# A linear-attention and MLP block on one core: tile 3 turned through memory, three tiles normalised on ScalarE, and the first tiles' small work put in other places

## The chip, the cores and the metric

The kernel runs on one core of one Trainium2 chip. The metric is the device time of one execution in microseconds (us), the median of several runs. A profile of one execution stands beside it; its times are those of the span from the first to the last instruction.

## The reference, cut to what matters

`x` has 2048 rows (tokens) of 512 floats. The rows are normalised, and two branches that both read the normalised rows are added to `x`:

```python
xn = layernorm(x)                                  # per row: (x - mean) / sqrt(var + 1e-5)
q, k, v = split(xn @ wqkv)                         # 32 heads of 16
phi = lambda t: where(t > 0, t + 1, exp(t)) + 1e-6
kv, z = phi(k)^T v, sum(phi(k))                    # per head, over all tokens
a = (phi(q) kv / (phi(q) z + 1e-6)) @ wo
b = relu(xn @ w1 + b1) ** 2 @ w2 + b2              # 512 -> 1376 -> 512
out = x + a + b
```

## The kernel before

**Tiles and stages.** The 2048 tokens are 16 tiles of 128 (`NT`), four to a block (`TB`). The change lies in the first stage, which goes over the tiles once. For each tile i this stage normalises the rows (`xp[i]`), turns them so that the features lie on the partitions, splits the turned tile into a rounded high part and a remainder (`xs..h`, `xs..l`), multiplies by the k weights (`project`, 12 matmuls of 128x512, line 368), applies phi (`phi_k`, lines 359 to 363), splits phi(k) the same way (`parts`, lines 375 and 376), splits the normalised rows themselves (`tokens`, `tok`, lines 111 and 119), and adds the product of tokens and phi(k) to four sums (`kx`, 12 matmuls, line 388). Splitting always means: ScalarE copies the high part, then VectorE (in `tokens` mostly GpSimd) subtracts it from the source. The later stages (from about 94 us on) make the MLP and the attention out of these results.

**Two ways to turn a tile.** Tiles below `NDVE` (0 to 3 before) are turned by four TensorE transposes against an identity (`turned_pe`, line 307), from PSUM. From `NDVE` on a tile is turned "by moves": `normalise` writes `xp[i]` in groups of 32 columns, `regroup` (line 280) stores it into a DRAM buffer `via`, `move` (line 288) loads it back in four pieces into `xg`, and `turn` (line 292) transposes 32x32 blocks on VectorE. Tiles 4 and 5 make the trip singly (`xg4s`, two places), tiles 6 and 7, 8 and 9 and so on in pairs. `transposed(i)` does either and gives back three pieces of work: `high` (line 323, ScalarE), `low` (line 326, VectorE) and `keep_t`, which stores the turned tile to DRAM as `xTd` for a later stage (line 335), for tiles below `NDVE` after a ScalarE copy out of PSUM.

**Statistics and normalising.** `measure` (lines 233 and 234, VectorE) gives mean and variance, `roots` (lines 244 and 245, GpSimd, the addition for tiles 0, 1 and 6 on VectorE) gives the inverse deviation. `normalise` works on VectorE for tiles below `NPE` = 8 (line 267); from 8 on it first makes `u = -mean * r` (line 253, VectorE) and gives back ScalarE work (`last`, line 257).

**Order.** There is no scheduler: the order of the calls is the order on each engine, and an engine works its queue strictly in order. All loads, stores and moves of this stage go through one queue, that of SP, also in order; an SP instruction that waits holds up all later ones. The lines 576 to 661 spell out tiles 0 to 3. The loop over i from 2 (line 806) then issues, per turn: `move()`, `project(i)`, for i < `NDVE` the turning of tile i + 1, `phi_k(i)` with `mid` (after its first ScalarE instruction) and `late` (after its second) as places for `high` and `low`, `parts(i)`, `tokens(i + 1)`, the put-off normalising `later`, the turning of tile i + 2, the statistics, and `kx(i - 1)`. `ones(i)` (line 345, GpSimd) sets the last feature column of a tile to 1 once nobody needs its value. `load_x` (line 158) loads raw rows: tiles 4 to 7 in one load, 8 to 15 in four loads of 512 KB.

TensorE's order between 16 and 40 us is thus: kx(0), the transposes of tile 3, kx(1), project(3), kx(2), project(4), kx(3), project(5), kx(4), project(6).

Of the kernel before, what the change touches and what calls it, by code (L numbers as in the profile page):

```python
# [7 lines left out]
F32 = mybir.dt.float32  # L8
F32R = mybir.dt.float32r
AF = mybir.ActivationFunctionType  # L10
OP = mybir.AluOpType
# [7 lines left out]
def kernel(  # L19
# [39 lines left out]
    BT = TB * P  # L59
    NF = -(-F // P)  # L60
    NPE = 2 * TB
    NDVE = NPE - 4
    WARM = 11
    NP = NF // 2
    FP = NF * P
# [25 lines left out]
    def two(name):  # L91
        return keep.tile([P, 2, 512], F32, name=name, tag=next_tag("x"))
# [7 lines left out]
    def f32(ap):  # L100
        return ap.bitcast(F32)
# [7 lines left out]
    def copy(eng, o, i, bias=0.0):  # L109
        if eng == "act":  # L110
            nc.scalar.activation(o, i, AF.Copy, bias=bias)  # L111
        elif bias:
            ENG[eng].tensor_scalar(o, i, bias, None, op0=OP.add)
        else:
            ENG[eng].tensor_copy(o, i)

    def split(h, l, src, eh, el):
        copy(eh, h, src)
        ENG[el].tensor_tensor(out=l, in0=src, in1=f32(h), op=OP.subtract)  # L119
# [36 lines left out]
    def load_x(i, t):  # L156
        n = t.shape[1]
        nc.sync.dma_start(t, xf[i * P:(i + n) * P, :].rearrange("(i p) d -> p i d", i=n))
        for k in range(n):
            xr[i + k] = t[:, k]  # L160
# [68 lines left out]
    def measure(g, *ks):  # L229

        tiles, st, mv, _ = g
        for k in ks or range(len(tiles)):
            nc.vector.bn_stats(st[:, k, :], xr[tiles[k]])  # L233
            nc.vector.bn_aggr(mv[:, k, :], st[:, k, :])

    def statistics(*tiles):
        g = group(*tiles)
        measure(g)
        return g

    def roots(tiles, st, mv, y):

        n = len(tiles)
        (nc.vector if tiles[0] in (0, 1, 6) else nc.gpsimd).tensor_scalar(y[:, 1, :n], mv[:, :n, 1], 1e-5, None, op0=OP.add)
        nc.gpsimd.tensor_tensor(out=y[:, 0, :n], in0=y[:, 1, :n], in1=power[:, :n], op=OP.pow)

    def normalise(tiles, st, mv, y):

        n = len(tiles)
        r, u = (y[:, k, :n] for k in range(2))  # L250
        if tiles[-1] >= NPE:

            nc.vector.scalar_tensor_tensor(u, mv[:, :n, 0], -1.0, r, op0=OP.mult, op1=OP.mult)
        later = []

        def last(i, o, src, k):
            nc.scalar.activation(o, src, AF.Identity, bias=u[:, k:k + 1], scale=r[:, k:k + 1])
            if i in groups:
                regroup(i)

        for k, i in enumerate(tiles):
            o, src = xp[i], xr[i]
            if i >= NDVE:

                o, src = o.rearrange("p g (j c) -> p g j c", j=NJ), gjc(src)
            if i < NPE:
                nc.vector.tensor_scalar(o, src, mv[:, k, 0:1], r[:, k:k + 1], op0=OP.subtract, op1=OP.mult)
                if i in groups:
                    regroup(i)
            else:  # L270
                later.append(lambda a=(i, o, src, k): last(*a))
        return later
# [12 lines left out]
    def move(n=8):  # L285
        for _ in range(n):
            if moves:
                nc.sync.dma_start(*moves.pop(0))
# [50 lines left out]
    def run(*what):  # L339
        for f in what:  # L340
            f()

    def ones(i):

        nc.gpsimd.memset(xp[i][:, D - 1:] if i < NDVE else xp[i][:, NJ - 1, P - 1:], 1.0)

    def tokens(i, el="pool"):
        tok[i] = pair(f"tok{i}")
        h, l = tok[i][:, 0], tok[i][:, 1]
        src = xp[i]  # L350
        if i >= NDVE:
            h, l, src = gjc(h), gjc(l), src.rearrange("p g (j c) -> p g j c", j=NJ)
        split(h, l, src, "act", el)
        if NDVE <= i + 1 < NT:
            ones(i + 1)

    def phi(ps, p, mid=lambda: None, late=lambda: None):

# [12 lines left out]
    def parts(i):  # L371

        p = kp[i]
        pk[i] = pair(f"pk{i}")
        copy("act", pk[i][:, 0], p, 1e-6)
        nc.vector.scalar_tensor_tensor(pk[i][:, 1], p, 1e-6, f32(pk[i][:, 0]), op0=OP.add, op1=OP.subtract)
# [168 lines left out]
    for i0 in range(0, NT, TB):  # L545
        a = first_xp[i0]
        for k in range(TB):
            xp[i0 + k] = a[:, k]
        if i0 + TB <= NDVE:
            continue  # L550
        n = TB if i0 >= NPE else TB // 2
        if i0 < NPE:
            single = work.tile([P, 2, 512], F32, name=f"xg{i0}s", tag="r0")
            for k in range(2):
                i = i0 + k
                xp[i], xg[i] = (t.rearrange("p (g n) -> p g n", g=NJ) for t in (xp[i], single[:, k]))
                groups[i] = [xp[i], xg[i]]
        o = work.tile([P, n, 512], F32, name=f"xg{i0}", tag="r0" if i0 + TB == NT else "r3" if i0 >= NPE else "rc")
        for k in range(0, n, 2):
            i = i0 + TB - n + k  # L560
            u, v = (t.rearrange("p a (g c) -> p (a g c)", g=NJ) for t in (a[:, TB - n + k:][:, :2], o[:, k:k + 2]))
            groups[i + 1] = [t.rearrange("p (g n) -> p g n", g=NJ) for t in (u, v)]
            u, v = (t.rearrange("p (g i c) -> p g i c", g=NJ, i=2) for t in (u, v))
            for m in range(2):
                xp[i + m], xg[i + m] = u[:, :, m], v[:, :, m]
# [53 lines left out]
    high1(1)  # L619
    heads_k(3)  # L620
    low1(1)
    for u in range(2):
        some(0, u, (2,))
    some(1, 0, (2,))
# [7 lines left out]
    keep0()  # L632
    keep1()
    rests_k("dve", 3)
    fourth = statistics(3)
    roots(*fourth)
    high, low, keep2 = transposed(2)
    high()
    low()
    rest(2)  # L640
    rest(3)
    load_x(8, x8[:, :2])
    load_x(10, x8[:, 2:])
    load_x(12, two("x12"))
    project(2, pks[2], wk, HL)
    single = group(4)
    soon = group(5)
    normalise(*fourth)
    load_x(14, two("x14"))
    phi_k(0, pks[0])  # L650
    measure(single)
    tokens(0)
    roots(*single)
    parts(0)
    phi_k(1, pks[1])
    normalise(*single)
    parts(1)
    tokens(1, "dve")
    measure(soon)
    roots(*soon)  # L660
    keep2()


# [142 lines left out]
    for i in range(2, NT):  # L806
        if i == 13:
            nc.sync.dma_start(b1s[:, :NF - 1], b1[:(NF - 1) * P].rearrange("(f p) -> p f", p=P))
            for a, o, n in units(NF - 1):
                nc.sync.dma_start(b1s[a:a + n, NF - 1:], b1[o:o + n, None])  # L810
        move()
        if i == 9:
            load_o()
        if i > 10:
            fetch()
        ps = pks[i] if i < 3 else bank(f"pk{i}")
        if i > 2:
            project(i, ps, wk, HL)
        high = low = keep_t = lambda: None
        if i < NDVE:  # L820
            high, low, keep_t = transposed(i + 1)
        later = normalise(*soon) if i == 3 else []

        soon_turned = transposed(i + 2) if 11 <= i and i + 2 < NT else ()

        def mid():
            high()
            more(i)

        def late():  # L830
            low()
            more(i)

        if i == 12:
            rawz = raw_1(NF - 1)
            T.update({n: tokens_sum(n, f"B{n - 1}") for n in (1, 2)})
        if i == 12:
            w = load_1("q", 0)
        if i == 13:
            todo_1 = operands_first(0, w)  # L840
            extra.append(todo_1.pop(1))
        if i == 14:
            z = pair("w1z0")
            extra.append(lambda: split(z[:, 0], z[:, 1], rawz, "act", "dve"))
            o34 = halves(four("Tf", "r0"))
            extra.extend(sums_of(xT[NB - 1], xT[NB - 2], *o34))
            lows = [extra.pop() for k in range(2)]
            extra += [todo_1[0], lows[1], todo_1[1], lows[0], *todo_1[2:]]
        phi_k(i, ps, mid, late)
        more(i)  # L850
        run(*soon_turned)
        if i != 3:
            later = normalise(*soon) if soon else []
        parts(i)
        keep_t()
        if i == 2:
            tokens(2)
        if i + 1 < NT:
            tokens(i + 1)
        run(*later)  # L860
        if NDVE < i + 2 < 13:
            run(*transposed(i + 2))
        pieces(int(i > 11))
        if i == 2:
            ahead[3] = statistics(6, 7)
        if i + 2 in (4, 6, 8, 10):
            ahead[i + 2] = group(i + 6, i + 7)
        if i < 10:
            measure(ahead[(i + 2) // 2 * 2], i % 2)
        soon = ahead.get(i + 1, ())  # L870
        if soon:
            roots(*soon)
        kx(i - 1)
        more(i)
# [499 lines left out]
```

## Time and profile before

| | |
|---|---|
| median of 3 runs | 410.01 us (409.84 to 410.3) |
| profiled execution | 410.38 us, span 408.7 us |
| TensorE matmuls busy | 402.7 us, 1943 instructions |
| VectorE busy | 308.9 us |
| ScalarE busy | 265.8 us |
| GpSimd busy | 48.4 us |
| granted TensorE clock | 1.00 throughout |

In the profile PE is a TensorE matmul, PEld its weight load, DVE is VectorE, ACT ScalarE, POOL GpSimd, and SPq the queue of SP. A row of the timeline gives start, duration, engine, line, operation, the output and input names, shapes, the count, and in brackets the idle time of the engine before it with what ended it. Matmuls are pipelined: one of 128x512 is shown with 0.39 us, but they follow each other every 0.227 us, 12 of them in 2.72 us. Instructions of the other engines overlap a little too, so the distance from start to start is the better measure of what one costs.

### The profile page before, as it was taken

The numbers are of one execution on the slowest core, as the hardware profiler recorded it, in microseconds if no ns is written. First come the engines' busy times: TensorE is split into PE (matmuls) and PEld (weight loads), VectorE is DVE, ScalarE is ACT, GpSimd is POOL, SyncE is SP. The second block draws the span as 40 slices with busy tenths as digits, with TensorE's granted clock in tenths as the row PEclk, the third lists the DMA queues.
The fourth block names the chain that finished last, engine by engine and source line by source line (L and its number), as shares of the span: only waits on it lengthen the run. The fifth ranks groups of instructions, "written<-read, shape, count | busy, mean of one in ns | idle before, by whom it ended". The sixth has DMA issues, their size and how long they took to land.

```text
span 408.7 us, 5625 instructions
## 1 busy us (share of the span) xinstructions
PE 402.7 (99%) x1943; PEld 331.0 (81%) x1943; DVE 308.9 (76%) x560; ACT 265.8 (65%) x463; POOL 48.4 (12%) x81
## 2 busy tenths in 40 slices
PE   7999999999999999999999999999999999999996
PEld 6878888888788888888878888888888888878885
DVE  6886666597898999988349997567989676449833
ACT  4656667556888789887728751677587857837520
POOL 5343333220000000030000300000000200001200
PEclk9999999999999999999999999999999999999999
DMA  6947326820332231381554912421121881024612
GB/s 212 363 151 227 130 105 206 236 48 0 102 108 79 78 103 27 86 217 33 186 223 150 209 32 102 117 53 51 51 79 36 227 198 29 2 102 154 105 26 103
DMA packets 46030, 48.48 MB, mean 119 GB/s; under 512 B 8177, under 2 KB 30449, under 8 KB 45746
## 3 DMA queue, kind: packets, MB, share of 16 engines
q1 hardware_dynamic: 43698, 43.93, 34.2%
q0 software_dynamic: 2304, 4.20, 6.5%
q8 instruction: 15, 0.25, 0.2%
q14 instruction: 13, 0.11, 0.1%
HBM read 37.49 MB, written 9.44 MB: 115 GB/s over the span
## 4 chain that ended last, share of the span: by engine, by line
PE 94%; DMA 2%; DVE 1%; ACT 1%; POOL 1%; SPq 0%; issue 0%; DVEq 0%
PE acc L130 37%; PE b L487 33%; PE pk L368 9%; PE kx L388 9%; PE acc L498 2%; PE pz L130 1%; DMA via<-xp 1%; DMA x<-in_A_x_dram 1%; PE b L130 1%; PE pz0b L130 1%; DMA xg4s<-via 0%; PE pt L307 0%; PE acc L505 0%; DVE st L233 0%; PE pkv L908 0%; POOL tok L119 0%
## 5 line engine op out<-in xcount | busy, mean ns | idle before, releaser
L130 PE MATMUL acc<-w2r,s 128*128 128x512 f32 x477 | 112.8, 390 | 0.0
L130 PEld LDWEIGHTS acc<-w2r,s 128*128 128x128 f32 x477 | 89.4, 188 | 19.2 <-issue 0.7
L487 PE MATMUL b<-T,aop 128*128 128x512 f32 x336 | 83.5, 390 | 0.0
L487 PEld LDWEIGHTS b<-T,aop 128*128 128x128 f32 x336 | 63.0, 188 | 13.9 <-ACT t L111 0.8
L1046 POOL DMA_DIRECT2D res<-in_B_b_dram x16 | 14.4, 1099 | 276.8 <-DVE dt L429 90.9
L388 PE MATMUL kx<-pk,tok 128*128 128x512 f32 x192 | 46.2, 390 | 0.0
L388 PEld LDWEIGHTS kx<-pk,tok 128*128 128x128 f32 x192 | 35.9, 188 | 7.5
L487 PE MATMUL b<-xs0h,aop 128*128 128x512 f32 x112 | 36.9, 390 | 0.0
L130 PE MATMUL acc<-mh,aTsr 128*128 128x512 f32 x112 | 35.7, 389 | 0.0
L1054 DVE TENSOR_TENSOR res<-acc,res 128x512 f32<-128x512 f32 x16 | 10.7, 689 | 20.5 <-PE acc L130 19.2
L111 ACT ACTIVATE aop<-S 128x512 fp32r<-128x512 f32 x28 | 17.5, 624 | 12.6 <-DVE S L727 12.6
L487 PEld LDWEIGHTS b<-xs0h,aop 128*128 128x128 f32 x112 | 21.0, 188 | 4.4
L130 PEld LDWEIGHTS acc<-mh,aTsr 128*128 128x128 f32 x112 | 21.0, 188 | 4.4
L119 POOL TENSOR_TENSOR tok<-xp,tok 128x512 fp32r<-128x512 f32 x15 | 19.8, 1320 | 39.2 <-ACT tok L111 39.2
L122 DVE TENSOR_TENSOR w2r<-r,w2r 128x512 fp32r<-128x512 f32 (+2 forms) x35 | 23.7, 681 | 0.5 <-ACT w2r L111 0.4
L119 DVE TENSOR_TENSOR aop<-S,aop 128x512 fp32r<-128x512 f32 x28 | 19.2, 687 | 4.8 <-ACT aop L111 4.4
L119 DVE TENSOR_TENSOR s<-c,s 128x512 fp32r<-128x512 f32 x20 | 13.5, 689 | 11.4 <-ACT s L111 11.3
L487 PE MATMUL b<-xs0l,aop 128*128 128x512 f32 x56 | 21.8, 389 | 0.0
L130 PE MATMUL acc<-ml,aTsr 128*128 128x512 f32 x56 | 21.8, 389 | 0.0
L111 ACT ACTIVATE w2r<-r 128x512 fp32r<-128x512 f32 x32 | 19.6, 619 | 2.6 <-DMA out_dram<-res 2.0
L487 PE MATMUL b<-xs1h,aop 128*128 128x512 f32 x56 | 19.5, 389 | 0.0
L111 ACT ACTIVATE T<-Tf 128x512 fp32r<-128x512 f32 x16 | 9.5, 624 | 14.4 <-DVE Tf L670 14.3
(194 smaller groups left out, 749.9 us busy)
## 6 DMA issues: line engine op xcount, KB each, us to landing
r<-in_B_w_dram SPq DMA_DIRECT2D x49, 256.0 KB, 3.1
res<-in_A_x_dram SPq DMA_DIRECT2D x8, 512.0 KB, 4.2
res<-in_B_b_dram POOLq DMA_DIRECT2D x16, 256.0 KB, 5.5
out_dram<-res SPq DMA_DIRECT2D x15, 256.0 KB, 2.1
via<-xp SPq DMA_DIRECT2D x5, 512.0 KB, 2.8
xg<-via SPq DMA_DIRECT2D x20, 128.0 KB, 2.8
xTd<-t SPq DMA_DIRECT2D x8, 256.0 KB, 3.3
x<-in_A_x_dram SPq DMA_DIRECT2D x4, 512.0 KB, 6.7
```

What stands on the lines that cost most here:

```text
L111: nc.scalar.activation(o, i, AF.Copy, bias=bias)
L119: ENG[el].tensor_tensor(out=l, in0=src, in1=f32(h), op=OP.subtract)
L122: nc.vector.tensor_tensor(out=l, in0=src, in1=f32(h), op=OP.subtract)
L130: nc.tensor.matmul(ps, lhsT=a[u], rhs=b[v], start=first and n == 0, stop=last and n == 2)
L368: nc.tensor.matmul(ps, lhsT=cols(i)[u][:, j, slot(i)], rhs=w[v][:, j, :], start=first and n == 0, stop=last and n == len(steps) - 1)
L388: nc.tensor.matmul(kxp[c], lhsT=tok[i][:, u, c * P:(c + 1) * P], rhs=pk[i][:, v], start=i == 0 and (u, v) == first, stop=i == NT - 1 and ( ...
L487: nc.tensor.matmul(ps, lhsT=a[u][:, j * P:(j + 1) * P], rhs=b[v][:, j, :], start=first and j == 0 and n == 0, stop=last and j == 1 and n == 2,
L498: nc.tensor.matmul(ps, lhsT=s[u][:, k * P:(k + 1) * P], rhs=w2s[NF - 1][u][:, a:z], start=first and u == 0, stop=stop and u == 1)
L1046: nc.gpsimd.dma_start(r[:, i], b2[None, :].partition_broadcast(P), accum_op=OP.add)
L1054: nc.vector.tensor_tensor(out=r[:, a:z], in0=ps, in1=r[:, a:z], op=OP.add)
```

## The change

The diff does the following:

- `NDVE` goes from 4 to 3: tile 3 is turned by moves. The buffer for single tiles gets three places, for tiles 3, 4 and 5.
- A new bound `NACT` = 5 takes the place of `NPE` in `normalise`: tiles 5, 6 and 7 are normalised on ScalarE. Tile 5 is normalised after `tokens(2)`; tiles 6 and 7 in `late` of turn 3, behind the high part of tile 4 and ahead of `tokens(3)`. In turn 3 `high` stands in `late`, no longer in `mid`.
- Statistics: those of tile 3 go ahead of tile 2's normalising, tile 5's into turn 2, tile 7's behind `parts(2)` and `tokens(2)`, tiles 8 and 9 both into turn 3.
- Tile 3 is normalised, stored and moved ahead of tile 2's transposes in the order of the calls.
- Loads: tile 8 and 9's stands behind tile 3's store and ahead of its moves, 10 and 11's behind tile 5's store, 12 and 13's behind tile 6 and 7's store, 14 and 15's in turn 4.
- `ones(3)` goes behind `tokens(0)`; `tokens` can put off its subtraction, so tile 1's copy precedes phi(k)'s copy of `parts(1)`.

```diff
-    NDVE = NPE - 4
+    NDVE = NPE - 5
+    NACT = NPE - 3
...
-        if tiles[-1] >= NPE:
+        if tiles[-1] >= NACT:
             nc.vector.scalar_tensor_tensor(u, mv[:, :n, 0], -1.0, r, op0=OP.mult, op1=OP.mult)
...
-            if i < NPE:
+            if i < NACT:
                 nc.vector.tensor_scalar(o, src, mv[:, k, 0:1], r[:, k:k + 1], op0=OP.subtract, op1=OP.mult)
...
-    def tokens(i, el="pool"):
+    def tokens(i, el="pool", now=True, ahead=True):
...
-        split(h, l, src, "act", el)
-        if NDVE <= i + 1 < NT:
+        copy("act", h, src)
+
+        def low():
+            ENG[el].tensor_tensor(out=l, in0=src, in1=f32(h), op=OP.subtract)
+
+        if now:
+            low()
+        if ahead and NDVE <= i + 1 < NT:
             ones(i + 1)
+        return low
...
-        if i0 + TB <= NDVE:
+        if i0 < TB:
             continue
...
-            single = work.tile([P, 2, 512], F32, name=f"xg{i0}s", tag="r0")
-            for k in range(2):
-                i = i0 + k
+            single = work.tile([P, 3, 512], F32, name=f"xg{i0}s", tag="r0")
+            for k in range(3):
+                i = i0 + k - 1
...
     low1(1)
+    fourth = statistics(3)
+    roots(*fourth)
...
     rests_k("dve", 3)
-    fourth = statistics(3)
-    roots(*fourth)
+    normalise(*fourth)
+    load_x(8, x8[:, :2])
+    move()
     high, low, keep2 = transposed(2)
     high()
     low()
     rest(2)
     rest(3)
-    load_x(8, x8[:, :2])
-    load_x(10, x8[:, 2:])
-    load_x(12, two("x12"))
     project(2, pks[2], wk, HL)
     single = group(4)
     soon = group(5)
-    normalise(*fourth)
-    load_x(14, two("x14"))
     phi_k(0, pks[0])
     measure(single)
     tokens(0)
+    ones(NDVE)
     roots(*single)
     parts(0)
     phi_k(1, pks[1])
     normalise(*single)
+    token_low = tokens(1, "dve", False)
     parts(1)
-    tokens(1, "dve")
-    measure(soon)
-    roots(*soon)
+    token_low()
     keep2()
...
-        if i < NDVE:
+        if i <= NDVE:
             high, low, keep_t = transposed(i + 1)
+        if i == 2:
+            measure(soon)
+            roots(*soon)
...
         def mid():
-            high()
+            if i != 3:
+                high()
             more(i)
 
         def late():
+            if i == 3:
+                high()
+                run(*later)
+                load_x(12, two("x12"))
+                tokens(3)
             low()
             more(i)
...
+        if i == 2:
+            ahead[3] = group(6, 7)
+            measure(ahead[3], 0)
         parts(i)
+        if i == 2:
+            tokens(2, ahead=False)
+            run(*later)
+            load_x(10, x8[:, 2:])
+            later = []
         keep_t()
-        if i == 2:
-            tokens(2)
-        if i + 1 < NT:
+        if 2 < i < NT - 1:
             tokens(i + 1)
-        run(*later)
-        if NDVE < i + 2 < 13:
+        if i != 3:
+            run(*later)
+        if i == 4:
+            load_x(14, two("x14"))
+        if NDVE < i + 1 < 12:
             run(*transposed(i + 2))
         pieces(int(i > 11))
         if i == 2:
-            ahead[3] = statistics(6, 7)
+            measure(ahead[3], 1)
...
-        if i < 10:
-            measure(ahead[(i + 2) // 2 * 2], i % 2)
+        if 2 < i < 10:
+            measure(ahead[(i + 2) // 2 * 2], *((0, 1) if i == 3 else (i % 2,)))
```

## The prediction

> **What bounds the kernel now.** I read the page's busy line first, then busy time by windows, then TensorE's waits in the first 100 us, then its instructions in order of time, and last the chain of waits, which says why it waited.
>
> ```profile
> PE 402.7 (99%) x1943; PEld 331.0 (81%) x1943; DVE 308.9 (76%) x560; ACT 265.8 (65%) x463; POOL 48.4 (12%) x81
> ```
> ```profile
> 31.50:102.00 70.50, 70.50 (x313) 58.34 (x311) 49.20 (x83) 44.81 (x76) 19.80 (x31) 1.00 0.44 133
> ```
> ```profile
> PE pk L368 <- ACT xs0h L323: 0.6, 1, 0.6
> ```
>
> TensorE is the bound: it has no gap from 31.5 us to the tail. Nothing gets faster unless TensorE gets less work or loses a wait. The one wait in the change's stretch is the 0.6 us in which project(4) waits for the high part of turned tile 4. So the change can gain only between 19 and 34 us, and it can lose wherever it makes an operand of TensorE later than now.
>
> ```profile
> 16.46 2.88 PE L388 MATMUL kx<-pk,tok 128*128 128x512 f32 x12
> 19.18 0.60 PE L307 MATMUL pt<-ident,xp 128*128 128x128 f32 x4
> 19.54 3.00 PE L388 MATMUL kx<-pk,tok 128*128 128x512 f32 x12
> 22.37 0.39 PE L368 MATMUL pk<-wkh,xs1h 128*128 128x512 f32 x1
> 25.09 2.88 PE L388 MATMUL kx<-pk,tok 128*128 128x512 f32 x12
> 28.61 0.50 PE L368 MATMUL pk<-wkh,xs0h 128*128 128x512 f32 x1 [0.64 <-ACT xs0h L323]
> ...
> 31.47 2.88 PE L388 MATMUL kx<-pk,tok 128*128 128x512 f32 x12
> ```
> ```profile
> 15.48 1.29 POOL tok L119
> ...
> 18.09 0.56 DVE xp L267
> 18.66 5.09 DMA via<-xp
> ...
> 23.82 0.34 SPq L288
> ...
> 25.15 1.92 DMA xg4s<-via
> ...
> 27.19 0.72 DVE t L292
> 27.93 0.64 ACT xs0h L323
> ...
> 28.61 3.02 PE pk L368 x12
> ```
>
> Two things are to be seen. A group of 12 matmuls takes 2.72 us when nothing disturbs it (16.46 to 19.18), so the distances beyond that are what can be won. And tile 4's trip through memory is the chain: normalised at 18.65, stored by 23.75 (5.09 us), moved back by 27.07 (3.25 us from the first move), turned and copied (0.74 from turn to copy, 0.68 from copy to matmul: 1.42 us from turn to project).
>
> **The gain, step by step.** (1) The four transposes of tile 3 go: kx(1) starts at 19.18 in place of 19.54, 0.36 us. (2) From kx(1) to project(3) it is 22.37 - 19.54 = 2.83 in place of 2.72: 0.11 us. (3) project(4) starts 28.61 - 25.09 = 3.52 after kx(2) in place of 2.72: 0.80 us, if tile 4 is early enough. (4) project(4) takes 31.47 - 28.61 = 2.86, because the first matmul after the wait is followed late: 0.14 us. The sum is 1.41 us at most. With no wait kx(1) then starts at 19.18, project(3) at 21.90, kx(2) at 24.62, project(4) at 27.34, kx(3) at 30.06, project(5) at 32.78, kx(4) at 35.50, project(6) at 38.22.
>
> The Trainium skill, "VectorE: DVE Perf Modes", section The three transpose paths, gives 390 ns for a TensorE transpose of 128x128 bf16. Four would make an estimate of 1.56 us in place of step (1) and a sum of 2.6; the row says 0.36, because they stream one behind another, and I go by the row.
>
> **Is every operand there in time?** This decides the rest, and I follow each chain with distances from these rows.
>
> ```profile
> 12.55 0.69 DVE L233 BATCH_NORM_STATS2 st<-x 128x6 f32<-128x512 f32 x1
> 13.27 0.18 DVE L234 BATCH_NORM_AGGREGATE mv<-st 128x2 f32<-128x6 f32 x1
> 13.54 0.69 DVE L326 TENSOR_TENSOR xs1l<-pt,xs1h 128x512 fp32r<-128x512 f32 x1
> ...
> 17.45 0.69 DVE L363 SCALAR_TENSOR_TENSOR k<-pk,k 128x512 f32<-128x512 f32 x1
> ...
> 19.45 0.69 DVE L119 TENSOR_TENSOR tok<-xp,tok 128x512 fp32r<-128x512 f32 x1
> 20.05 0.69 DVE L233 BATCH_NORM_STATS2 st<-x 128x6 f32<-128x512 f32 x1
> ...
> 20.88 0.66 DVE L326 TENSOR_TENSOR xs1l<-pt,xs1h 128x512 fp32r<-128x512 f32 x1
> ...
> 25.85 0.64 DVE L244 TENSOR_SCALAR y<-mv 128x2 f32<-128x2 f32 x1
> ...
> 31.68 0.71 DVE L292 STREAM_TRANSPOSE t<-xg4s 128x512 f32<-128x512 f32 x1 [0.30 <-issue]
> ...
> 37.90 0.71 DVE L292 STREAM_TRANSPOSE t<-xg 128x512 f32<-128x512 f32 x1 [1.33 <-DMA xg<-via]
> ```
> ```profile
> 18.18 0.63 ACT L111 ACTIVATE pk<-k 128x512 fp32r<-128x512 f32 x1 [0.76 <-DVE k L363]
> 18.72 0.62 ACT L111 ACTIVATE tok<-xp 128x512 fp32r<-128x512 f32 x1
> ...
> 36.27 1.51 ACT L257 ACTIVATE xp<-x,y 128x512 f32<-128x512 f32 x2
> ```
> ```profile
> 10.13 1.28 SPq L335 DMA_DIRECT2D xTd<-t  x2
> 11.47 3.94 SPq L158 DMA_DIRECT2D x<-in_A_x_dram  x4
> ...
> 25.68 0.38 SPq L280 DMA_DIRECT2D via<-xp  x1
> ...
> 27.80 1.73 SPq L288 DMA_DIRECT2D xg4s<-via  x4
> 29.63 0.38 SPq L280 DMA_DIRECT2D via<-xp  x1
> 30.05 2.88 SPq L335 DMA_DIRECT2D xTd<-t  x2
> 33.03 2.02 SPq L288 DMA_DIRECT2D xg<-via  x4
> ```
> ```profile
> via<-xp SPq DMA_DIRECT2D x1, 512.0 KB, 2.8
> ```
>
> *Tile 3.* Its statistics (0.8 us) move ahead of tile 2's normalising on VectorE, which delays that by some 0.3 to 0.45 us; by the rows VectorE had the same 0.8 us behind it (12.55 to 13.4), so tile 3's normalising takes just that place and ends near 13.4, and low(2) starts at 13.54 as before. The store is issued at 13.4. Ahead of it on SP stand only the two xTd stores (10.13 to 11.41); the four loads that began at 11.47 now come later. So I take the 2.8 us of the 512 KB store at 29.63 rather than the 5.09 of tile 4's, which had those loads ahead: stored by 16.2; plus 3.25, moved by 19.5. VectorE is free for the turn at 20.05 (0.60 after tok of tile 1). The latest start that costs nothing is 21.90 - 1.42 = 20.48. Cover: 0.4 us on VectorE, 1.0 on the trip. With 5.09 the trip ends at 21.8 and costs 1.35. The load of tiles 8 and 9 sits between store and moves on SP (0.5 us of issue, beside the wait for the store, so nothing), but its 512 KB go ahead of the moves' data.
>
> *On GpSimd* ones(3) is queued between tok(0) (done 16.77) and the roots of tile 4; it needs tile 3's store landed (16.2), so it costs its 0.1 us; were it 18.5, tile 4's normalising behind it on VectorE would be late, and with it phi(k) of tile 1.
>
> *ScalarE, turn 2.* tok(1) moves into the 0.76 us idle ahead of 18.18: free. The copy of turned tile 3 out of PSUM (line 111) is gone.
>
> *Tile 4.* Normalised at 18.7, stored with 2.8 (lower bound 2.1, tile 5's gap between store at 25.68 and first move at 27.80) by 21.5, moved by 24.8. VectorE reaches its turn later: turn(3) 20.05, statistics of 5 at 20.7, low(3) 21.5, phi(2) 22.1, u of 5, statistics of 6, remainder of pk(2), statistics of 7 (0.6 + 0.15 + 0.83 + 0.6 + 0.83) end at 25.1, y another 0.15 to 0.64. Turn at 25.3 to 25.8, project(4) possible at 26.7 to 27.2, needed at 27.34. So step (3) is won, with 0.1 to 0.6 us to spare.
>
> *ScalarE, turn 3.* Behind high(4) (26.0 to 26.5) come tiles 6 and 7 (1.51), tok(3) and then pk(3), which kx(3) needs at 30.06: 0.54 for each of the two copies (18.18 to 18.72), 0.63 for pk: 3.22, so 29.2 to 29.7. Spare 0.4 to 0.9.
>
> *Tile 5.* Normalised on ScalarE (0.76 us, half of 1.51) behind tok(2): phi(2) 22.1, pk(2) 0.73 later, two copies of 0.54, so done near 24.6. Before, its store was issued only at 25.68, because SP stood behind tile 4's moves. Those now end near 23.2 (1.73 for four), so the store goes at 24.6; stored with 2.1 to 2.8, moved with 3.25: 30.0 to 30.7. The load of 10 and 11 and tile 3's xTd lie ahead of the moves, so no lower. I take turn(5) at 30.3 (31.68 before); project(5) possible at 31.7, needed at 32.78.
>
> *phi(4).* Two statistics in place of one stand ahead of it on VectorE: turn(5) 30.3, low(5) 1.42 later, 0.60 for it, twice 0.83, phi(4) at 34.0; pk(4) starts 0.73 later (18.18 less 17.45) and takes 0.63: 35.35 against 35.50. It costs nothing, just so.
>
> *Tile 6, the narrow place.* On SP tile 5's turned store follows turn(5), then the moves of 6 and 7. They began 1.35 us after the turn (33.03 - 31.68), and turn(6) began 4.87 us after them (37.90, waiting 1.33 for them). With turn(5) at 30.3: 31.65, 36.5, project(6) possible at 37.95, needed at 38.22. Spare 0.27, and the load of tiles 12 and 13 (512 KB) now lies ahead of them.
>
> ```profile
> 15.00:16.00 1.00, 1.00 (x6) 0.79 (x5) 1.00 (x3) 0.76 (x2) 0.52 (x1) 1.00 1.02 358
> ```
>
> 512 KB at 358 GB/s, what the loads of x got in this window, are 1.46 us. That is the upper bound of the added delay; nothing is the lower one. The load is issued about 2.5 us before the moves, so most of it should be through: I take 0.5, a third, and less the 0.27 to spare a wait of 0.2 us. The other loads are issued long before their statistics (8 and 9 near 14 us for 32, 10 and 11 near 25 for turn 4, 14 and 15 near 34 for turn 7) and cost nothing. After that, tiles 7 and 8 onward have the same order as before, and no gap from 31.5 on says that their cover is the same.
>
> The Trainium skill, "DMA: Bandwidth & Descriptors", section Queues, rings and completion order, says that each DMA engine takes descriptors in ring order. By that rule the load's data goes wholly ahead of the moves' as far as it is not through, at most a wait of 1.2 us and 409.8; the trace agrees so far that tile 4's store behind the loads took 5.09 us against 2.8.
>
> **The sum.** -0.36 - 0.11 - 0.80 - 0.14 + 0.2 = -1.2 us. The profiled execution took 410.38 (span 408.7 and 1.7 around it), so 409.2; from the median of 410.01 it is 408.8.
>
> **The rivals.** A measurement of this kernel can tell about 0.2%, 0.8 us, from no change.
>
> - *Tile 6 eats the gain.* The moves of 6 and 7 come late by most of the load's 1.46 us; with 0.27 to spare project(6) waits 0.8 to 1.2: 409.4 to 409.8. For it: turn(6) waits for these very moves already. Against it: SP issues the load well ahead.
> - *The trips stay as long as tile 4's, slower.* The queue is as full as before, only later: loads of 8, 10 and 12 now lie among the moves. With 8.4 us a trip (18.66 to 27.07) tile 3 is there at 21.8 (1.35 late) and tile 5 at 24.6 + 1.35 + 8.4 = 34.35 against 31.36 + 1.35 (1.65 late): 3.0 - 1.4 gives 411.6. It decides against the change once the lateness of all trips adds up to over 2.2 us, that is from about 8 us a trip. Against it: 5.09 was measured with four loads ahead, and 2.8 without. The Trainium skill, "VectorE: DVE Perf Modes", section Rules for kernel authors, prefers TensorE for a 128x128 transpose; if the trips are long, the trace would side with it.
> - *ScalarE becomes the bound in turn 3.* high(4) half a microsecond later than above makes pk(3) and project(4) late by 0.3 to 0.6: 409.1 to 409.4.
> - *It doesn't do what it says.* Tile 4's moves wait on something else than the loads and arrive as before; then only (1) and (2) are won: 409.5.
>
> **How the numbers follow.** Forecast (a gain of 0.9 to 1.4 us, 408.6 to 409.1): 0.55. Tile 6: 0.22. Long trips: 0.11. ScalarE: 0.07. Not doing it: 0.05. Faster by over 0.8 us (under 409.2): 0.55 + 0.05 of ScalarE's = 0.60; slower: 0.11; the same: the remaining 0.29. The likeliest is 408.8; 408.4 to 410.0 leaves out the long trips and little else.
>
> **What would show it.** Right: no transposes between kx(0) and kx(1); project(3) near 21.9, project(4) near 27.3 with no idle time, tile 3's store landing in under 3 us, TensorE's order after 40 us 1.2 us earlier throughout. Wrong: an idle PE row with ACT xs1h ahead of project(3) (trip of tile 3), with ACT pk ahead of kx(3) or kx(4) (ScalarE or VectorE too full), or ahead of project(6) with turn(6) waiting for the moves (the load of 12 and 13).

## The result, and the profile after

The changed kernel takes 411.17 us (median of 6 runs, 410.8 to 411.62), the kernel before 409.92 in the same comparison (6 runs, 409.36 to 410.34): ratio 1.0034, 95% interval 1.0023 to 1.0045. It is slower by 1.25 us where 1.2 us less was forecast. The profiled execution took 410.8 us, span 409.1.

TensorE in order of time, after the change (start, duration, line, operation; the rows that begin a group):

```profile
16.36 5.64 PE L396 MATMUL kx<-pk,tok 128*128 128x512 f32 x24
21.83 0.39 PE L376 MATMUL pk<-wkh,xs1h 128*128 128x512 f32 x1
...
24.55 2.88 PE L396 MATMUL kx<-pk,tok 128*128 128x512 f32 x12
27.27 0.39 PE L376 MATMUL pk<-wkh,xs0h 128*128 128x512 f32 x1
...
29.99 2.90 PE L396 MATMUL kx<-pk,tok 128*128 128x512 f32 x12
32.91 0.51 PE L376 MATMUL pk<-wkh,xs0h 128*128 128x512 f32 x1
...
36.49 3.02 PE L396 MATMUL kx<-pk,tok 128*128 128x512 f32 x12 [0.52 <-ACT pk L112]
39.65 0.50 PE L376 MATMUL pk<-wkh,xs0h 128*128 128x512 f32 x1
...
42.49 2.94 PE L396 MATMUL kx<-pk,tok 128*128 128x512 f32 x12
```

kx(0) and kx(1) are one run of 24 matmuls, the transposes are gone, and up to kx(3) every group starts within 0.1 us of the forecast (21.90, 24.62, 27.34, 30.06). Then it is lost: project(5) starts 0.13 us late, kx(4) at 36.49 where 35.50 was to be had, project(6) at 39.65 where it was 38.22. In the first profile of the kernel before project(6) started at 39.63: everything won is gone by tile 6.

VectorE of the changed kernel shows what was late:

```profile
31.48 0.71 DVE L293 STREAM_TRANSPOSE t<-xg4s 128x512 f32<-128x512 f32 x1 [0.76 <-DMA xg4s<-via]
...
33.51 0.69 DVE L234 BATCH_NORM_STATS2 st<-x 128x6 f32<-128x512 f32 x1
...
34.33 0.66 DVE L234 BATCH_NORM_STATS2 st<-x 128x6 f32<-128x512 f32 x1
...
35.12 0.66 DVE L371 SCALAR_TENSOR_TENSOR k<-pk,k 128x512 f32<-128x512 f32 x1
...
38.22 0.71 DVE L293 STREAM_TRANSPOSE t<-xg 128x512 f32<-128x512 f32 x1 [1.05 <-DMA xg<-via]
```

turn(5) waits for its moves until 31.48 (forecast 30.3); the two statistics and phi(4) behind it are late by as much, so pk(4) is, and kx(4) waits 0.52. turn(6) waits 1.05 us for the moves of 6 and 7, until 38.22. The queue of SP shows what lay beside these moves, here with the issues and, from the DMA view, the landing of the last of tile 5's moves and of the store of 6 and 7:

```profile
24.61 0.34 SPq L281 DMA_DIRECT2D via<-xp  x1
24.99 0.43 SPq L159 DMA_DIRECT2D x<-in_A_x_dram  x1
25.47 0.53 SPq L336 DMA_DIRECT2D xTd<-t  x1
26.80 1.80 SPq L289 DMA_DIRECT2D xg4s<-via  x4
28.70 0.38 SPq L281 DMA_DIRECT2D via<-xp  x1
29.12 0.43 SPq L159 DMA_DIRECT2D x<-in_A_x_dram  x1
29.65 3.09 SPq L336 DMA_DIRECT2D xTd<-t  x2
32.84 2.04 SPq L289 DMA_DIRECT2D xg<-via  x4
```
```profile
xg4s<-via SPq DMA_DIRECT2D x1, 64.0 KB, 2.8
```
```profile
via<-xp SPq DMA_DIRECT2D x1, 512.0 KB, 4.0
```

Tile 5's store itself was quick (moves issued 2.2 us after it, as forecast), but its last move needed 2.8 us instead of 1.9, with the 512 KB of tiles 10 and 11 issued 1.8 us ahead of the first move. The store of 6 and 7 needed 4.0 instead of 2.8, with that load ahead of it and the load of 12 and 13 right behind it; with only one of the two it took 3.3 and 3.1, with neither 2.8 to 3.2 (profiles of the experiments below). Its end, at 32.7, is not by itself what set the moves of 6 and 7 back: ahead of them on SP also stands the store of turned tile 5 (the second of the two at 29.65), which waits for turn(5) and is issued by 32.74.

**The other half.** 410.38 us, the execution profiled before, lies above all six runs of the comparison, and of the 81 runs of this kernel beside the experiments below only three lie above 410.3. Two more profiles of the kernel before (409.64 and 409.61 us) show what an ordinary execution does; TensorE, and tile 4's store, of the first of these:

```profile
25.05 2.88 PE L388 MATMUL kx<-pk,tok 128*128 128x512 f32 x12
27.77 0.46 PE L368 MATMUL pk<-wkh,xs0h 128*128 128x512 f32 x1
```
```profile
via<-xp SPq DMA_DIRECT2D x1, 256.0 KB, 3.2
```

The store takes 3.2 us (3.0 in the other) and not 5.09, and project(4) follows kx(2) by 2.72: there is no wait to be won. Why the store was slow in the first profile is not shown.

A measure that leaves the rest out is the time from the start of kx(0) to the start of kx(5), nine groups, 24.48 us if nothing waits. From kx(7) to the end of the span the five profiles in the table agree within 0.3 us. Ahead of kx(0) profiles differ, whatever the kernel: it starts at 16.16 to 16.91 us in all those taken here, and why is not shown.

| kernel | kx(0) to kx(5), us, one profile each |
|---|---|
| before | 25.89 (the first), 25.11, 25.10 |
| changed | 26.13, 26.56 |

So an ordinary execution had 0.63 us to win and not 1.41, and the change lost 1.65 to 2.08.

### The profile page after: what moved, and what is told of

Read it like the earlier page. It is cut to its first block, busy times and chain, and to the rows that moved or that the text cites. A ratio compares the mean times of both kernels' runs of the same rounds, so it can differ in the third digit from the quotient of the medians.

```text
span 409.1 us, 5635 instructions
## 1 busy us (share of the span) xinstructions
PE 403.7 (99%) x1939; PEld 331.3 (81%) x1939; DVE 308.9 (76%) x560; ACT 267.7 (65%) x465; POOL 49.6 (12%) x81
## 4 chain that ended last, share of the span: by engine, by line
PE 91%; DMA 3%; DVE 2%; ACT 1%; SPq 1%; issue 1%; DVEq 0%; ACTq 0%
PE acc L131 37%; PE b L495 33%; PE pk L376 8%; PE kx L396 7%; PE acc L506 2%; PE pz L131 1%; DMA xg<-via 1%; DMA xg4s<-via 1%; DMA x<-in_A_x_dram 1%; SPq L289 1%; PE b L131 1%; PE pz0b L131 1%; DMA via<-xp 1%; DVE k L371 1%; DVE t L293 1%
```

## The experiments

The queue theory: the change lays the loads of tiles 10 to 13 among the trips of tiles 5 to 7, and their data holds up the moves. Its first rival, the VectorE theory: the second statistic ahead of phi(4) makes pk(4) late, and the rest follows. Each kernel is timed against the kernel before on its chip (409.65 to 409.77 us in all comparisons below).

**The changed kernel again** (no edit).

> The changed kernel once more, without an edit, since its six runs lie between 410.8 and 411.6 and its profile was taken at the fast end of them. Queue theory (the loads of tiles 10 to 13 lie ahead of the moves of tiles 5 to 7): the time varies with how long the loads hold the moves up; project(6) again starts at 39.6 us or up to 0.8 later, with turn(6) waiting for the moves. VectorE theory (the second statistic ahead of phi(4) is the cause): kx(4) waits 0.5 us or more for pk(4), and project(6) follows it by 2.72 us without a wait of its own. Time 410.8 to 411.6 by both.

411.22 us, 1.0040 (1.0028 to 1.0053). kx(4) waits 0.55 us, and project(6) has a wait of its own, 0.58, for the high part of tile 6. Against the VectorE theory, which gave project(6) none.

**Late loads.**

Tiles 10 and 11 go behind the moves of 6 and 7, 12 and 13 into turn 4, 14 and 15 into turn 6.

```diff
         move()
+        if i == 4:
+            load_x(10, x8[:, 2:])
...
-                load_x(12, two("x12"))
...
-            load_x(10, x8[:, 2:])
...
-        if i == 4:
-            load_x(14, two("x14"))
+        if i in (4, 6):
+            load_x(i + 8, two(f"x{i + 8}"))
```

> Only the places of three loads are changed: tiles 10 and 11 behind the moves of 6 and 7, 12 and 13 in turn 4, 14 and 15 in turn 6. Queue theory: tile 5's moves land near 30, turn(5) at 30.2 to 30.5 in place of 31.5, the moves of 6 and 7 land by 36.5 in place of 38.1, project(6) starts at 38.2 to 38.5, and the time falls by 1.3 to 2.5 us, to 408.6 to 409.5, below the kernel before. VectorE theory: two statistics still stand ahead of phi(4), kx(4) still waits 0.5 us, and at most 0.5 us is won.

410.02 us, 1.0013 (1.0004 to 1.0022): 1.2 us below the changed kernel beside it, still above the kernel before. kx(0) to kx(5) is 24.96, and VectorE's two turns are earlier:

```profile
31.10 0.70 DVE L293 STREAM_TRANSPOSE t<-xg4s 128x512 f32<-128x512 f32 x1
...
37.30 0.71 DVE L293 STREAM_TRANSPOSE t<-xg 128x512 f32<-128x512 f32 x1 [0.45 <-DMA xg<-via]
```

kx(0) of this profile starts 0.47 us later than the changed kernel's (16.83 against 16.36), so counted from there turn(5) is 0.85 us earlier and turn(6) 1.39. The loads' places alone give back most of the loss. The time missed the expected 408.6 to 409.5, which was counted from a gain of 1.41 us, 0.78 of it not there in an ordinary execution.

**The statistics alone.**

```diff
+        if i == 3:
+            ahead[4] = group(8, 9)
+            measure(ahead[4], 0)
         parts(i)
+        if i == 3:
+            measure(ahead[4], 1)
...
-        if 2 < i < 10:
-            measure(ahead[(i + 2) // 2 * 2], *((0, 1) if i == 3 else (i % 2,)))
+        if 3 < i < 10:
+            measure(ahead[(i + 2) // 2 * 2], i % 2)
```

> Only the statistics of tiles 8 and 9 are moved, into VectorE's idle time before and after the remainder of pk(3), so that none stands between low(5) and phi(4); the loads stay where the change put them. VectorE theory: kx(4) no longer waits, project(6) follows without a gap, and the change's gain appears: 408.8 to 409.6. Queue theory: kx(4) starts 0.5 us earlier, but turn(6) still waits for the moves of 6 and 7 until about 38.2, project(6) still starts near 39.6, and the time stays within 0.3 us of the changed kernel.

411.34 us, 1.0040 (1.0028 to 1.0053). kx(4) follows project(5) by 2.85 and does not wait; project(6) waits 1.00 for tile 6:

```profile
40.25 0.50 PE L376 MATMUL pk<-wkh,xs0h 128*128 128x512 f32 x1 [1.00 <-ACT xs0h L324]
```

The VectorE theory falls: its wait is real, but taking it away only lengthens the next one.

**The kernel before with late loads** (10 and 11 behind the moves of 6 and 7, 12 and 13 in turn 4, 14 and 15 in turn 6).

> The kernel before, tile 3 still turned on TensorE, with only the loads put late: 10 and 11 behind the moves of 6 and 7, 12 and 13 in turn 4, 14 and 15 in turn 6. Queue theory: tile 4's store lands in under 3 us in place of 5.1, project(4) loses its wait (0.8 and 0.14 us), and this half of the forecast gain comes without the change: 409.0 to 409.3. VectorE theory: VectorE has turn(4) late anyway (27.2 us, behind the statistics of 6 and 7), so at most 0.3 us is won.

410.14 us, 1.0012 (1.0003 to 1.0021): slower, where both theories had it faster. project(4) has no wait, but in ordinary executions it had none before. New is a wait of 0.25 at project(6): turn(6) starts at 37.64 against 37.21 in the kernel before, though the moves began at the same time (32.04 and 32.10). I took this for the load right behind the moves (issued at 34.11), so that not only a load ahead but any load next to the moves would cost. The profiles do not settle that. From the first move of 6 and 7 to turn(6) it is 5.60 us here, and 4.87 to 5.11 in the three profiles of the kernel before, which has no load there. But in the changed kernel with the same load behind the moves it is 4.86 (late loads) and 4.61 (late loads and moved statistics, below), no longer than without any load near (4.66 and 4.77 in the eighth kernel, below).

**The kernel before, twice more** (no edit, one execution each).

> The kernel before, unchanged, profiled a second time: the first profile's 410.38 us is above all of the 21 runs beside it (median 409.65), so project(4)'s wait in it may be larger than usual. From the start of kx(0) to the start of kx(5) the first profile has 25.89 us, 24.48 of it matmuls; 1.41 is what I called the gain. If the first profile was a long one, this span is 25.0 to 25.6 here, and the gain to be had was only 0.5 to 1.1 us. If it was ordinary, 25.8 to 26.0 again, and the 0.7 us are in the start before 16.4 us.

> The same once more, for the spread: the start of kx(0) between 16.2 and 16.9 as in the other profiles, and the span from kx(0) to kx(5) as in the second profile within 0.3 us if it is a property of the kernel, and spread over 0.5 us or more if it hangs on how the loads happen to flow.

409.64 and 409.61 us; 25.11 and 25.10. The first profile was a long one, and of the 1.41 us that I called the gain 0.78 are its own.

**Late loads and moved statistics** (the second and third edits together).

> The late loads of the second experiment and the moved statistics of tiles 8 and 9 together. Queue theory: the loads were the main cause, the statistics add the rest; from kx(0) to kx(5) 24.5 to 24.8 us against 24.96 with late loads alone, the time 0.2 to 0.4 us below that, 409.6 to 409.9. VectorE theory: with the loads gone phi(4) is the last wait, so this one gives the larger part, 0.5 us or more.

410.56 us, 1.0022 (1.0013 to 1.0031), 25.45: not better than late loads alone, rather worse (the intervals overlap), a miss for both theories. The statistic of tile 9 now stands ahead of turn(5), which starts at 31.66 in place of 31.10, and project(6) waits 0.22.

**Early loads** (all three behind tile 3's moves, ahead of tile 4's store).

```diff
     load_x(8, x8[:, :2])
     move()
+    load_x(10, x8[:, 2:])
+    load_x(12, two("x12"))
+    load_x(14, two("x14"))
...
-                load_x(12, two("x12"))
...
-            load_x(10, x8[:, 2:])
...
-        if i == 4:
-            load_x(14, two("x14"))
```

> The changed kernel with all three loads (10 and 11, 12 and 13, 14 and 15) issued early, right behind tile 3's moves and ahead of tile 4's store. Queue theory: the wait goes where the loads go: tile 4's store lands after 4.5 to 5.5 us in place of 2.0, turn(4) at 27.0 or later, project(4) waits 0.8 to 1.3 us for xs0h; but turn(5) comes no more than 0.3 after its project could use it and project(6) does not wait for the moves. In all 410.0 to 411.0. VectorE theory: kx(4) waits as in the changed kernel, on top of project(4)'s wait: 411.5 or more.

416.58 us, 1.0163 (1.0140 to 1.0185). The wait does go where the loads go, and is larger than expected. The landing of tile 4's store, TensorE's waits from 20 to 60 us, and its windows (span, busy time of PE, PEld, DVE, ACT and POOL, then the granted clock, DMA share, GB/s):

```profile
via<-xp SPq DMA_DIRECT2D x1, 256.0 KB, 7.7
```
```profile
PE pk L376 <- ACT xs0h L324: 4.4, 1, 4.4
```
```profile
32.00:34.00 2.00, 1.73 (x4) 1.44 (x5) 1.29 (x2) 2.00 (x4) 0.00 (x0) 0.50 0.35 100
34.00:36.00 2.00, 2.00 (x6) 1.52 (x6) 1.30 (x2) 1.09 (x3) 1.31 (x2) 0.50 0.85 314
```

The store lands after 7.7 us behind 1.5 MB, project(4) waits 4.40, and then runs at half the granted clock, 6 matmuls where 2 us hold 9 at 0.227 us each. So the time lost is more than the wait alone.

**One load at a time**: tiles 12 to 15 late, 10 and 11 left; then 10 and 11 behind the moves of 6 and 7, 12 to 15 left.

> Of the late loads only those of tiles 12 and 13 (to turn 4) and 14 and 15 (to turn 6); 10 and 11 stay ahead of tile 5's moves. Queue theory, load by load: turn(5) stays at 31.5 and kx(4) keeps its wait of about 0.5 us, but turn(6) comes at 37.3 to 37.6 in place of 38.2, and about half of the second experiment's gain appears: 410.4 to 410.8. If the load of 12 and 13 is the whole cause, 410.0; if it is none of it, 411.2.

> Of the late loads only that of tiles 10 and 11, put behind the moves of tiles 6 and 7; 12 and 13 stay ahead of those moves. Queue theory, load by load: turn(5) at 31.1 and with it kx(4) a little earlier, but the load of 12 and 13 still lies ahead of the moves of 6 and 7, so turn(6) stays at 37.9 to 38.2: 410.6 to 411.0. If the load of 10 and 11 is the whole cause, 410.0.

The first: 410.83 us, 1.0027 (1.0017 to 1.0037), 25.98; turn(5) at 31.63 and kx(4) waiting 0.56 as expected, turn(6) at 38.25 and not 37.5, because its moves stand behind tile 5's turned store and so behind turn(5). The second: 411.57 us, 1.0042 (1.0028 to 1.0056), where 410.6 to 411.0 was expected; turn(5) at 30.66 and no wait at kx(4), but the moves of 6 and 7 lie between two loads, and in the profile VectorE waits for them longer than in any other kernel:

```profile
39.61 0.71 DVE L293 STREAM_TRANSPOSE t<-xg 128x512 f32<-128x512 f32 x1 [3.21 <-DMA xg<-via]
```

The profiled execution took 413.75 us, though, and the five others of this kernel 411.05 to 411.76: it is as little an ordinary one as the first profile was, and how long VectorE waits in the others is not shown.

So neither load is the whole cause by the times: with either one moved the kernel stays 1.06 and 1.80 us above the kernel before. That the load of 10 and 11 makes turn(5) late is shown: counted from the start of kx(0) it comes after 15.07 to 15.12 us in the three profiles with that load ahead and the change's statistics, and after 14.27 and 14.29 in the two with the load elsewhere. For the load of 12 and 13 the profiles show less. With it ahead of the moves of 6 and 7 it is 5.38 and 5.77 us from the first of them to turn(6) (the changed kernel's two profiles), and 5.26 without it; and the second kernel did not take the load of 10 and 11 away but put it behind those moves.

**Loads out of the way** (10 and 11 in turn 4 behind the store of 8 and 9, 12 and 13 in turn 5, 14 and 15 in turn 7; the statistics of tile 8 ahead of the remainder of pk(3), those of 10 and 11 both in turn 5; the expectations call it the eighth kernel).

```diff
-                load_x(12, two("x12"))
...
+        if i == 3:
+            measure(ahead[4], 0)
         parts(i)
...
-            load_x(10, x8[:, 2:])
...
-        if i == 4:
-            load_x(14, two("x14"))
+        if i in (4, 5, 7):
+            n = {4: 10, 5: 12, 7: 14}[i]
+            load_x(n, x8[:, 2:] if n == 10 else two(f"x{n}"))
...
-        if 2 < i < 10:
-            measure(ahead[(i + 2) // 2 * 2], *((0, 1) if i == 3 else (i % 2,)))
+        if 2 < i < 10 and i != 4:
+            measure(ahead[(i + 2) // 2 * 2], *((0, 1) if i == 5 else (i % 2,)))
```

> All three loads out of the way of the trips of tiles 5 to 7: 10 and 11 in turn 4 behind the store of 8 and 9, 12 and 13 in turn 5, 14 and 15 in turn 7; the statistics of 8 in VectorE's idle time ahead of the remainder of pk(3), those of 10 and 11 both in turn 5. Queue theory: no data but the trips' own is on the queue from 18 to 38 us; turn(5) at 31.0, turn(6) at 36.9 or earlier, from kx(0) to kx(5) 24.6 to 24.9 us against 25.1 of the kernel before, time 409.2 to 409.6. Rival (the longer order on SP, not the loads' data, holds the moves: the store of turned tile 5 waits for turn(5) and stands ahead of them): turn(6) stays at 37.3 or later, 409.8 to 410.2.

409.56 us, 0.9992 (0.9983 to 1.0001): not told apart from the kernel before, its interval below that of late loads alone. VectorE's two turns:

```profile
30.58 0.70 DVE L293 STREAM_TRANSPOSE t<-xg4s 128x512 f32<-128x512 f32 x1
...
36.58 0.71 DVE L293 STREAM_TRANSPOSE t<-xg 128x512 f32<-128x512 f32 x1 [1.06 <-DMA xg<-via]
```

Both are early enough now, 0.9 and 1.6 us before the changed kernel's. The rival, that SP's longer order by itself holds turn(6) to 37.3 or later, fails here: the order stands, the moves of 6 and 7 still begin 1.34 us after turn(5), and turn(6) comes at 36.58. kx(0) to kx(5) is 24.61: nothing but 0.13 us is left of the waits.

**Stores behind the moves** (also the stores of turned tiles 3, 4 and 5 put behind the next moves).

> The same, and the stores of turned tiles 3, 4 and 5 put behind the next moves on SP, so that the moves of 6 and 7 wait for their own store only. Rival: this is what was missing: the moves of 6 and 7 begin at 31.5 to 31.9 in place of 32.4 or later, turn(6) at 36.2, project(6) without a wait, from kx(0) to kx(5) 24.5 to 24.7 us, time 409.0 to 409.4 and 0.3 to 0.8 below the eighth kernel. Queue theory alone: the same as the eighth kernel within 0.2.

409.71 us, 1.0001 (0.9992 to 1.0010), 25.24: no better. Tile 3's store was now issued directly ahead of the store of 6 and 7, whose moves could begin only 3.9 us after it (29.37 to 33.23), and turn(6) came at 37.49. Taking the turned stores out of the moves' way gains nothing if one of them then stands ahead of the tiles' own store; a kernel that avoids both was not run.

**Which part is the change's own?** The kernel before with the eighth kernel's loads, and the eighth kernel again beside it.

> The kernel before, tile 3 on TensorE, with the loads as in the eighth kernel: 10 and 11 in turn 4 behind the store of 8 and 9, 12 and 13 in turn 5, 14 and 15 in turn 7, the statistics of 10 and 11 both in turn 5. If the eighth kernel's gain comes from tile 3's turning, this one stays at the kernel before (409.5 to 409.9, from kx(0) to kx(5) 25.0 to 25.2 us) and 0.1 to 0.5 above the eighth. If it comes from the loads, this one has it too: 409.2 to 409.6.

> The eighth kernel once more, on the same chip as the kernel with only its loads: 409.2 to 409.8, from kx(0) to kx(5) 24.6 to 25.1 us; at or below both kernels. If tile 3's turning is worth its 0.36 us and the two matmuls that come sooner behind it, it lies 0.3 to 0.5 us below the other.

409.69 us, 1.0000 (0.9992 to 1.0009), 25.20; and 409.33 us, 0.9991 (0.9982 to 1.0000), 24.64. The loads' new places give the kernel before nothing. The changed kernel with them lies 0.36 us below in the same comparison, though its interval (0.9982 to 1.0000) overlaps the other's and just touches no change; that is near the 0.47 us forecast for the four transposes of tile 3, and no run has these alone.

## Why the prediction was wrong

- **Steps (1) and (2), the transposes: right.** kx(1) follows kx(0) without a gap and project(3) comes at 21.83; the last two kernels put it at some 0.36 us against the 0.47 forecast, with the change's other parts in it.
- **Step (3), tile 4's wait: not there.** Its 0.80 us were taken from one execution, whose 410.38 us already stood above the three runs shown. In two others tile 4's store lands in 3.2 and 3.0 us behind the same four loads, not in 5.09, and project(4) does not wait. Step (4)'s 0.14 us is there (project(4) takes 2.85 and 2.81), but without a wait ahead of it, so the reason given for it does not hold. From kx(0) to kx(5) the two profiles leave 0.63 in all.
- **Tiles 3 and 4, GpSimd, ScalarE: right.** The stores of 3 and 4 landed in 2.4 and 2.0 us (2.8 taken), and kx(3) starts at 29.99. The rival "ScalarE becomes the bound" did not come.
- **Tile 5: the step that failed.** The prediction saw the load of 10 and 11 ahead of the moves and wrote "so no lower"; it charged nothing for it above its own range and took turn(5) at 30.3. The store was as forecast, but from the first move to turn(5) it was 4.68 us (26.80 to 31.48) in place of 3.25. With the load out of the way turn(5) came at 30.58 and did not wait for its moves. "It costs nothing, just so" for phi(4) had 0.15 us to spare; it came at 35.12 in place of 34.0. On TensorE this is 1.06 of the 1.65 us: project(5) follows kx(3) by 2.92 and kx(4) follows project(5) by 3.58, each in place of 2.72.
- **Tile 6: the right place, and 1.43 us late in place of 0.2.** Most of it is turn(5) again: the moves of 6 and 7 began 1.36 us after it, as forecast (1.35), so they were late by the same 1.2. From there to turn(6) it was 5.38 us, and 5.77 in the second profile, in place of 4.87. That is 0.5 to 0.9 more, so the 0.5 charged here was near in size, though it is not shown that the load of 12 and 13 is the reason. What the term rested on, turn(5) in time, did not hold.
- **The sum.** -0.63 in place of -1.41, and +1.65 to 2.08 in place of +0.2: +1.0 to +1.5 by the profiles, +1.25 measured. The lateness is the larger part of the miss, the gain that was not there the smaller. The forecast's own slower rival, trips as long as tile 4's, had 0.11 and 411.6; the time came near it, but through the moves of tiles 5 to 7 and not through the single stores (2.0 to 2.4 us in the profile after), and tile 3 was in time.

Ring order, which the prediction cited from the Trainium skill, "DMA: Bandwidth & Descriptors", section Queues, rings and completion order, agrees with the early loads (7.7 us behind 1.5 MB). Why the kernel before lost 0.5 us by late loads stays open (turn(6) at 37.64 against 37.21, one profile each), as does why the changed kernel with late loads measured 0.37 us above the kernel before. In its profile the loss lies ahead of kx(0), which starts at 16.83 against 16.40 and 16.49, and kx(0) to kx(5) is shorter (24.96 against 25.1).

## What to carry to other kernels

Before a wait of half a microsecond is counted as a gain, see that the profiled execution is an ordinary one: compare its own time with all runs beside it, and take a second profile if it lies outside them. The same holds for the profile of an experiment. A bulk load is not free because its own data is needed late; on the shared queue here it was paid by the short transfers behind it, so it belongs where no chain of store, move and use is under way. Where several steps each have 0.1 to 0.3 us to spare and hang on one another, one late transfer takes them all.

## What the runs showed of the hardware

A wait of TensorE costs more than its length once it is long. In the kernel with early loads the granted clock fell to 0.50 with project(4)'s wait of 4.40 us, and from the start of project(4) to the start of kx(3) it was 5.29 us in place of 2.72. All four executions of this kernel have a mean clock of 0.99 to 0.996 over the span, where those of the changed kernel have 0.999 or 1.0. In the profiled execution of the kernel with only 10 and 11 late, a wait of 2.29 us at project(6) was enough; TensorE's windows of that profile:

```profile
40.00:42.00 2.00, 0.96 (x4) 0.83 (x5) 1.30 (x3) 1.61 (x3) 0.00 (x0) 0.98 0.99 334
42.00:44.00 2.00, 2.00 (x7) 1.52 (x6) 1.27 (x4) 0.98 (x3) 0.00 (x0) 0.50 0.83 204
```

From project(6) (41.04) to kx(5) (45.48) it is 4.44 us. The other five executions of this kernel have a mean clock of 0.998 to 1.0 against 0.994 here and are about 2 us shorter, so this is one execution of six. The clock did not fall when the wait began: here it fell near 41.9, 3.2 us after the wait began and 0.9 after work had begun again, and in the kernel with early loads near 31.6, 3.7 us after the wait began and still within it. The waits of 0.2 to 1.0 us in the other kernels left the clock at 1.00. The Trainium skill, "TensorE: Matmul & The Clock Gate", section Why this matters for your kernels, gives gaps of over some 3 us as what to avoid; here 2.29 us did it in one profile.
